# Linear attention block on one core: products of Wv with the state in two column tiles of TensorE

## The chip, the cores and the metric

The kernel runs on one core of one Trainium2 chip. The metric is the device time of one execution in microseconds (us); lower is better. A time given for a kernel is the median of several runs of it.

## The reference

x has 2048 rows of 640 columns, in bf16. There are 32 heads of 20 columns each. With phi(t) = (t + 1 if t > 0, else exp(t)) + 1e-6, the block computes, per head:

```
qkv = x @ wqkv                     # q, k, v: 640 columns each
pq, pk = phi(q), phi(k)
kv  = sum over rows of pk^T v      # 20 x 20 per head, the state
z   = sum over rows of pk          # 20 per head
o   = (pq @ kv) / (pq . z + 1e-6)
out = o @ wo                       # the heads side by side, 640 x 640
```

## The kernel before, in words

The kernel never forms v. Since v = x Wv, the state of all heads is Wv^T (x^T pk), of which only the 20 x 20 blocks on the diagonal are wanted. And since out = o wo, each head's state is multiplied with its 20 rows of wo once ("fold"), so that the end of the kernel is a single product of the normalized pq with a folded matrix of 640 x 640.

The stages on TensorE, in order:

1. Six products that only keep TensorE busy (L280), ten transposes of x (L198), then k = x Wk in 16 row tiles of 128 (L292). Exp on ScalarE (L305) and two operations on VectorE (L307, L310) make pk of it.
2. P = x^T pk (L319), 640 x 640, summed over the 16 row tiles, in two halves of 320 columns. Each half is copied out of PSUM into `pt` by ScalarE (L331) and VectorE (L334). In between stand tiles of q (L345), 20 in all, 128 columns by 512 rows of x each, with exp on ScalarE (L353) and two operations on VectorE (L357, L360) that make pq. VectorE also sums z (L366, L387), and the denominators' weighted sums (`wsum`, L412, four multiply-adds on VectorE behind one on ScalarE, L408, for each of the four blocks of 512 rows).
3. `kv_group` (L416, its products at L423): Wv^T P on the diagonal. The heads are taken in six groups `g`, five of six heads (GW = 120 columns) and one of two heads (40 columns). For each group five products are summed, one for each 128 rows of Wv: a weight of 128 x 128 (120 columns of Wv and 8 more), and 120 moving columns of `pt`. Groups 0 to 3 go to PSUM bank 0, groups 4 and 5 to bank 1.
4. `kv_mask` (L433, operations at L440): three VectorE operations multiply the results with a mask `bm` of diagonal blocks of 20 x 20 and write them as bf16 to `kvt`: groups 0 to 3 (480 columns), group 4 (120), group 5 (40).
5. `w2_group` (L444, products at L447), the fold: for each group two products of `kvt`'s 120 x 120 with the group's 120 rows of wo (`wog`), 320 columns each. A copy to `w2g` (L451) and a small DMA (L459) put the rows where the last stage wants them, in `w2p`.
6. The output (L487): pq times `w2p` for 16 row tiles, with the last denominators (`den`, L465; L470, L472) and normalizations (L479) in between, copies out of PSUM (L509, L512, L524), and the output DMAs.

The order on each engine is that of the program, written by hand. `P.add` records an operation for an engine with what it reads and writes. An operation waits, by semaphores, for the last writer of what it reads and for all readers of what it overwrites. The names count here, not the bytes: `("bank", b)` stands for a whole PSUM bank, `("kvt", g)` for one group. The product loop of one `P.add` signals once, with its last product. `next_q` issues a tile of q; an argument `between` is called after its exp was recorded and before its two VectorE operations, so that what it issues stands ahead of those in VectorE's queue and behind the tile's five products on TensorE. `todo` is a list of small operations (`work` fills it with weighted sums "w" and normalizations "n"), of which `pop` and `next_q(n)` take the next few. So around the state the order on TensorE is: tile of q, 30 products L423, tile of q, four products L447, tile of q, and so on. On VectorE it is: copies L334, three multiply-adds L412, three masks L440, then the two operations of the tile of q.

`pool_const` prepares constants on GpSimd (L167: zeros in `kvt`'s last group; L168: zeros in the last group of `wog`; the mask `bm` by two selections, L159). `load_rest` issues the DMA loads of Wq, x, Wv and wo (L260: five groups of 120 rows of wo) on SyncE's queue.

Of the kernel before, what the change touches and what calls it, by code (L numbers as in the profile page):

```python
# [7 lines left out]
ALU = mybir.AluOpType  # L8
# [74 lines left out]
def bass_standalone__linear_attn_block__prompt_kernel(nc, x, wqkv, wo, out):  # L83
    B, S, D = x.shape
    assert (B, S, D) == (1, 2048, 640)
    H, DH = 32, 20
    NC_ = D // 128
    NT = S // 128
    HALF = D // 2
    NSB = S // 512  # L90
    GW, NG = 120, 6
    gsz = [min(GW, D - GW * g) for g in range(NG)]
    BK = 512

    with contextlib.ExitStack() as ctx:
        es = ctx.enter_context

        def sb(name, cols, dt=BF16):
            return es(nc.sbuf_tensor(name, [128, cols], dt))
# [6 lines left out]
        wv = sb("wv", NC_ * D + 128)  # L106
        wog = sb("wog", NG * D)
# [4 lines left out]
        pt = sb("pt", NC_ * D)  # L112
        kvt = sb("kvt", NG * GW)
# [8 lines left out]
        bm = sb("bm", GW)  # L122
# [7 lines left out]
        ps = es(nc.psum_tensor("ps", [128, 8 * BK], F32))  # L130

        P = Plan(nc, es)

        def bank(b, n=BK, off=0, parts=128):
            return ps[0:parts, BK * b + off:BK * b + off + n]

        def two_banks(b, n=HALF, parts=128):
            return ps[0:parts, BK * b:BK * b + 2 * BK].rearrange(
                "p (g j) -> p g j", j=BK)[:, :, 0:n]

        def fold(ap, j=HALF):
            return ap.rearrange("p (g j) -> p g j", j=j)


        def pool_const():
            P.add("pool", lambda e: e.memset(ident[:, :], 0.0), writes=["ident"])
            P.add("pool", lambda e: e.affine_select(
                out=ident[:, :], in_=ident[:, :], pattern=[[-1, 128]], base=0,
                channel_multiplier=1, compare_op=ALU.not_equal, fill=1.0),
                reads=["ident"], writes=["ident"])  # L150
            P.add("dve", lambda e: e.memset(ones[:, :], 1.0), writes=["ones"])
            P.add("dve", lambda e: e.memset(eps[:, :], 1e-6), writes=["eps"])
            P.add("pool", lambda e: e.memset(wv[:, NC_ * D:], 0.0), writes=["wvpad"])
            P.add("pool", lambda e: e.memset(hm[:, :], 1.0), writes=["hm"])

            def band(t, pat, base, mult, name):

                v = t.rearrange("p (a b) -> p a b", b=pat[1][1])
                P.add("pool", lambda e: e.affine_select(  # L159
                    out=v, in_=v, pattern=pat, base=base, channel_multiplier=mult,  # L160
                    compare_op=ALU.is_ge, fill=0.0), reads=[name], writes=[name])


            band(hm[:, :], [[-4, 32], [0, 4]], 0, 1, "hm")
            band(hm[:, :], [[4, 32], [0, 4]], 3, -1, "hm")

            P.add("pool", lambda e: e.memset(kvt[:, 5 * GW:], 0.0), writes=[("kvt", 5)])  # L167
            P.add("pool", lambda e: e.memset(wog[:, 5 * D:], 0.0), writes=["wog5"])  # L168
            P.add("pool", lambda e: e.memset(bm[:, :], 1.0), writes=["bm"])
            for lo in (True, False):  # L170
                band(bm[:, :], [[-DH if lo else DH, NG], [0, DH]],
                     0 if lo else DH - 1, 1 if lo else -1, "bm")


        NPE = 2
# [48 lines left out]
        def w_cols(dst, lo, hi, col, key, eng):  # L224
            P.add(eng, lambda e: e.dma_start(
                dst[:, 0:NC_ * D].rearrange("p (c n) -> p c n", n=D)[:, :, lo:hi],
                wqkv[:, col + lo:col + hi].rearrange("(c p) n -> p c n", p=128)),
                writes=[key], dma=True)

        def load_xn(a, b, eng, reads=()):  # L230
            P.add(eng, lambda e: e.dma_start(
                xn[:, a * D:b * D].rearrange("p (t n) -> p t n", n=D),
                x[0, 128 * a:128 * b, :].rearrange("(t p) n -> p t n", p=128)),
                reads=reads, writes=[("xn", t) for t in range(a, b)], dma=True)
# [20 lines left out]
        def load_rest():  # L255
            w_cols(wqn, 0, D, 0, "wqn", "sp")
            for a, b in ((2, 6), (6, 11), (11, 16)):
                load_xn(a, b, "sp")
            w_cols(wv, 0, D, 2 * D, "wv", "sp")
            P.add("sp", lambda e: e.dma_start(  # L260
                wog[0:GW, 0:5 * D].rearrange("p (g n) -> p g n", n=D),
                wo[0:5 * GW, :].rearrange("(g p) n -> p g n", p=GW)),
                writes=["wog"], dma=True)
            P.add("sp", lambda e: e.dma_start(
                wog[0:gsz[5], 5 * D:6 * D], wo[5 * GW:D, :]), writes=["wog5"], dma=True)

# [148 lines left out]

        def kv_group(b):  # L416

            for lo, hi, bb in ((0, 4, b), (4, 6, b + 1)):
                def mm(e, lo=lo, hi=hi, bb=bb):
                    for g in range(lo, hi):  # L420
                        n = gsz[g]
                        for d in range(NC_):
                            r = e.matmul(  # L423
                                bank(bb, n, off=128 * (g - lo)),
                                wv[:, d * D + GW * g:d * D + GW * g + 128],
                                pt[:, d * D + GW * g:d * D + GW * g + n],
                                start=(d == 0), stop=(d == NC_ - 1))
                    return r
                P.add("pe", mm, reads=["wv", "wvpad"] + [("pt", d, h) for d in range(NC_)
                                                         for h in range(2)],  # L430
                      writes=[("bank", bb)])

        def kv_mask(b):  # L433
            for lo, n, bb, w in ((0, 4, b, GW), (4, 1, b + 1, GW), (5, 1, b + 1, 40)):
                src = ps[0:w, BK * bb + 128 * (lo % 4):BK * bb + 128 * (lo % 4) + 128 * n] \
                    .rearrange("p (g j) -> p g j", j=128)[:, :, 0:w]
                m = bm[0:w, 0:w].unsqueeze(1).broadcast_to([w, n, w])
                dst = kvt[0:w, GW * lo:GW * (lo + n)].rearrange(
                    "p (g j) -> p g j", j=GW)[:, :, 0:w]
                P.add("dve", lambda e, src=src, m=m, dst=dst: e.tensor_tensor(  # L440
                    dst, src, m, ALU.mult), reads=[("bank", bb), "bm"],
                    writes=[("kvt", g) for g in range(lo, lo + n)])

        def w2_group(g, b, eng="act"):  # L444
            n = gsz[g]
            for h in range(2):
                P.add("pe", lambda e, h=h: e.matmul(  # L447
                    bank(b + h, HALF, parts=GW), kvt[0:GW, GW * g:GW * (g + 1)],
                    wog[0:GW, g * D + HALF * h:g * D + HALF * (h + 1)], start=True, stop=True),
                    reads=[("kvt", g), "wog", "wog5"], writes=[("bank", b + h)])  # L450
            P.add(eng, lambda e: (e.copy if eng == "act" else e.tensor_copy)(  # L451
                fold(w2g[0:n, g * D:(g + 1) * D]), two_banks(b, parts=n)),
                reads=[("bank", b), ("bank", b + 1)], writes=[("w2g", g)])
            w2_rows(g)

        def w2_rows(g):

            w = gsz[g] // NC_
            P.add("sp", lambda e: e.dma_start(  # L459
                w2p[24 * g:24 * g + w, :].rearrange("p (c n) -> p c n", n=D),  # L460
                w2g[0:gsz[g], g * D:(g + 1) * D]),
                reads=[("w2g", g)], writes=[("w2p", g)], dma=True)
# [84 lines left out]
        for k in order.split():  # L547
            st = int(k[1])
# [20 lines left out]
        def take():  # L569
            small.append(small.pop(0))  # L570
            return small[-1]

        def next_q(n=1, between=None):
            q_tile(*qs.pop(0), take(), between)
            for _ in range(n):
                if todo:
                    todo.pop(0)()

        def inverse(s):
            b = take()  # L580
            den(s, b)
            den_act(s, b)
# [8 lines left out]
        def pop(n):  # L591
            for _ in range(n):
                todo.pop(0)()
# [15 lines left out]
        for st in range(NT - 2):  # L609
            p_step(1, st)  # L610
            if st in (0, 1):
                zst.pop(0)()
            if st == 5:
                z_finish(take())
                work("w0", "w1", "n0")
                pop(3)
            if st in (1, 4, 7, 10, 12):
                next_q({7: 2, 10: 2}.get(st, 0))
            if st == 11:
                inverse(0)  # L620
        assert not zst
# [1 line left out]
            p_step(1, NT - 2, (d,))  # L623
            p_step(1, NT - 1, (d,))
        p_out(1)
        pop(3)

        def state_groups():
            kv_group(0)
# [73 lines left out]
```

## Time and profile before

| | |
|---|---|
| median of 3 runs | 99.46 us (99.34 to 99.53) |
| the profiled execution | 99.4 us |
| its span, first to last instruction | 98.1 us |
| TensorE busy | 95.0 us (97% of the span) |
| VectorE busy | 74.0 us |
| ScalarE busy | 50.3 us |
| GpSimd busy | 3.5 us |
| mean granted TensorE clock | 1.000 |

Times within the trace count from the span's start. PE is TensorE's products, PEld its weight loads, DVE is VectorE, ACT ScalarE, POOL GpSimd, SPq SyncE's DMA queue. L423 is line 423 of the kernel. A product's record lasts longer than the step to the next product, since products follow each other through the array before the first has ended: for the time that a group of products takes on the engine, the steps from start to start count, not the records' lengths. Some records of products are missing from the trace (95 of 100 at L345, for instance).

### The profile page before, as it was taken

The numbers are of one execution on the slowest core, as the hardware profiler recorded it, in microseconds if no ns is written. First come the engines' busy times: TensorE is split into PE (matmuls) and PEld (weight loads), VectorE is DVE, ScalarE is ACT, GpSimd is POOL, SyncE is SP. The second block draws the span as 40 slices with busy tenths as digits, with TensorE's granted clock in tenths as the row PEclk, the third lists the DMA queues.
The fourth block names the chain that finished last, engine by engine and source line by source line (L and its number), as shares of the span: only waits on it lengthen the run. The fifth ranks groups of instructions, "written<-read, shape, count | busy, mean of one in ns | idle before, by whom it ended". The sixth has DMA issues, their size and how long they took to land.

```text
span 98.1 us, 1667 instructions
## 1 busy us (share of the span) xinstructions
PE 95.0 (97%) x651; PEld 62.4 (64%) x657; DVE 74.0 (75%) x138; ACT 50.3 (51%) x83; POOL 3.5 (4%) x15
## 2 busy tenths in 40 slices
PE   6999999999999999999999999999999999999991
PEld 2667777777777666555566556755447776677771
DVE  0305987888889897999849759999979998819332
ACT  5107454445698201462042476289796749665321
POOL 6800000000000000000000000000000000000000
DMA  2986899989999920000000000006600223322534
GB/s 47 361 193 131 162 169 135 218 272 379 366 362 284 205 63 10 0 0 0 0 7 0 0 0 0 0 0 165 164 15 0 98 102 134 134 70 73 197 134 134
DMA packets 17236, 11.73 MB, mean 120 GB/s; under 512 B 9933, under 2 KB 17229, under 8 KB 17229
## 3 DMA queue, kind: packets, MB, share of 16 engines
q1 hardware_dynamic: 16653, 11.10, 42.9%
q10 hardware_dynamic: 576, 0.53, 1.6%
q8 instruction: 5, 0.08, 0.4%
q14 instruction: 2, 0.02, 0.1%
HBM read 5.90 MB, written 2.62 MB: 87 GB/s over the span
## 4 chain that ended last, share of the span: by engine, by line
PE 90%; DVE 6%; ACT 1%; issue 0%
PE ps L292 23%; PE ps L487 22%; PE ps L345 21%; PE ps L319 17%; DVE za L366 3%; PE ps L280 3%; PE ps L447 2%; PE ps L423 1%; DVE pq L360 1%; ACT eq L353 1%; PE ps L198 1%; PE ps L465 1%; DVE eq L357 1%; DVE pt L334 0%; DVE osb L512 0%
## 5 line engine op out<-in xcount | busy, mean ns | idle before, releaser
L319 PE MATMUL ps<-pk,xn 128*128 128x320 bf16 x160 | 24.0, 299 | 0.0
L345 PE MATMUL ps<-xT,wqp 128*128 128x512 bf16 x95 | 23.1, 379 | 0.3
L292 PE MATMUL ps<-wk,xT 128*128 128x320 bf16 x160 | 22.9, 305 | 0.0
L487 PE MATMUL ps<-w2p,pq 128*128 128x320 bf16 (+3 forms) x170 | 22.3, 291 | 0.1
L353 ACT ACTIVATE eq<-ps 128x512 bf16<-128x512 f32 x20 | 11.9, 597 | 19.2 <-PE ps L345 19.0
L319 PEld LDWEIGHTS ps<-pk,xn 128*128 128x128 bf16 x160 | 15.6, 98 | 7.5
L292 PEld LDWEIGHTS ps<-wk,xT 128*128 128x128 bf16 x160 | 15.9, 100 | 6.5 <-ACT xT L210 0.2
L487 PEld LDWEIGHTS ps<-w2p,pq 128*128 128x128 bf16 x170 | 15.9, 98 | 6.4 <-DVE pq L479 0.2
L305 ACT ACTIVATE ek<-ps 128x640 bf16<-128x640 f32 x16 | 11.2, 704 | 11.8 <-PE ps L292 11.1
L345 PEld LDWEIGHTS ps<-xT,wqp 128*128 128x128 bf16 x100 | 9.7, 97 | 9.2
L360 DVE SCALAR_TENSOR_TENSOR pq<-ps,eq 128x512 bf16<-128x512 f32 x20 | 13.8, 692 | 0.7
L310 DVE SCALAR_TENSOR_TENSOR pk<-ps,ek 128x640 bf16<-128x640 f32 x16 | 13.2, 825 | 0.5
L412 DVE SCALAR_TENSOR_TENSOR ua<-pq,zc,ua 128x512 f32<-128x512 bf16 x12 | 9.0, 749 | 1.1 <-ACT ua L408 0.9
L307 DVE TENSOR_SCALAR ek<-ek 128x640 bf16<-128x640 bf16 x16 | 5.2, 324 | 5.9 <-ACT ek L305 5.9
L479 DVE TENSOR_TENSOR pq<-pq,rd 128x512 bf16<-128x512 bf16 x20 | 7.4, 418 | 2.8 <-ACT rd L472 2.8
L357 DVE TENSOR_SCALAR eq<-eq 128x512 bf16<-128x512 bf16 x20 | 5.8, 289 | 4.1 <-ACT eq L353 3.9
L524 ACT CAST osb<-ps 128x640 bf16<-128x640 f32 x9 | 6.2, 688 | 3.6 <-PE ps L487 3.4
L512 DVE CAST osb<-ps 128x320 bf16<-128x320 f32 (+2 forms) x8 | 3.5, 434 | 3.3 <-PE ps L487 3.1
L366 DVE TENSOR_TENSOR za<-pk 128x1280 f32<-128x1280 bf16 x4 | 5.8, 1483 | 0.0
L509 ACT CAST osb<-ps 128x320 bf16<-128x320 f32 (+1 forms) x8 | 3.1, 404 | 4.7 <-PE ps L487 4.5
L366 DVE TENSOR_TENSOR za<-za 128x1280 f32<-128x1280 f32 x3 | 4.4, 1482 | 0.0
L270 ACT COPY wqp<-wqn 128x640 bf16<-128x640 bf16 x5 | 4.3, 933 | 0.0
(41 smaller groups left out, 43.5 us busy)
## 6 DMA issues: line engine op xcount, KB each, us to landing
out_dram<-osb SPq DMA_DIRECT2D x15, 160.0 KB, 1.8
xn<-in_x_dram SPq DMA_DIRECT2D x2, 800.0 KB, 10.1
wqn<-in_wqkv_dram SPq DMA_DIRECT2D x1, 800.0 KB, 6.4
wv<-in_wqkv_dram SPq DMA_DIRECT2D x1, 800.0 KB, 13.6
wog<-in_wo_dram SPq DMA_DIRECT2D x1, 750.0 KB, 14.2
w2p<-w2g SPq DMA_DIRECT2D x5, 150.0 KB
xn<-in_x_dram SPq DMA_DIRECT2D x1, 640.0 KB, 7.6
wk<-in_wqkv_dram SPq DMA_DIRECT2D x3, 160.0 KB, 3.4
```

What stands on the lines that cost most here:

```text
L292: r = e.matmul(bank(b + h, HALF), xT[:, c * S + 128 * st:c * S + 128 * st + 128], wk[:, c * D + HALF * h:c * D + HALF * (h + 1)], start=(c ...
L305: P.add("act", lambda e: e.activation(fold(t[:, :]), two_banks(b), ACTF.Exp), reads=banks + ["table"], writes=[("ek", st % 3)])
L310: P.add("dve", lambda e: e.scalar_tensor_tensor(fold(pk[:, st * D:(st + 1) * D]), two_banks(b), 0.0, fold(t[:, :]), ALU.max, ALU.add), rea ...
L319: r = e.matmul(bank(d, HALF), xn[:, st * D + 128 * d:st * D + 128 * d + 128], pk[:, st * D + HALF * h:st * D + HALF * (h + 1)], start=(st ...
L345: r = e.matmul(bank(b), wqp[:, d * D + 128 * c:d * D + 128 * c + 128], xT[:, d * S + BK * sbk:d * S + BK * (sbk + 1)], start=(d == 0), sto ...
L353: P.add("act", lambda e: e.activation(t[:, :], bank(b), ACTF.Exp), reads=[("bank", b), "table"], writes=[("eq", i)])
L357: P.add("dve", lambda e: e.tensor_scalar(t[:, :], t[:, :], 1.0, 1e-6, ALU.min, ALU.add), reads=[("eq", i)], writes=[("eq", i)])
L360: P.add("dve", lambda e: e.scalar_tensor_tensor(pq[:, c * S + BK * sbk:c * S + BK * (sbk + 1)], bank(b), 0.0, t[:, :], ALU.max, ALU.add), ...
L366: P.add("dve", lambda e: e.tensor_tensor(d_ap, a, b, ALU.add), reads=ra + rb, writes=[dst])
L412: P.add("dve", lambda e: e.scalar_tensor_tensor(dst[:, :], v, z, a[:, :], ALU.mult, ALU.add), reads=[("pq", s, c), "zc", key], writes=[dkey])
L479: P.add("dve", lambda e: e.tensor_tensor(v, v, rd[i][:, BK * o:BK * (o + 1)], ALU.mult), reads=[("rd", sbk), ("pq", sbk, c)], writes=[("pq ...
L487: r = e.matmul(bank(b, hi - lo), pq[:, c * S + 128 * st:c * S + 128 * st + 128], w2p[:, c * D + lo:c * D + hi], start=(c == 0), stop=(c == ...
```

## The change

The products of Wv with the state are made in halves of the array. Each group of six heads is cut in two parts `t` of three heads, 60 columns. Part 0 takes 64 columns of weights and writes PSUM rows 0 to 63, part 1 takes 64 columns and writes rows 64 to 127; the moving operand is 60 columns of `pt`. The instructions alternate between the two parts. The last group of two heads has part 0 alone. So there are 55 products (50 with 60 columns, 5 with 40) in place of 30 (25 with 120, 5 with 40). All of them go to bank 0, 64 columns a group, in one recorded operation.

The mask operations become: part 0 of groups 0 to 4 (64 rows, 300 columns), part 1 of groups 0 to 4 (64 rows, 300 columns), group 5 (64 rows, 40 columns). Each of the first two writes part of every group 0 to 4.

`kvt` thus holds a group's heads in rows 0 to 59 and 64 to 123, and the fold's products sum over 128 rows in place of 120. `kvt` is zeroed as a whole at the start (720 columns in place of 120). `wog` is loaded in two DMAs of 64 rows in place of one of 120; the rows that belong to no head of the group meet zeros in `kvt`. The mask `bm` is made by two selections of the same size as before with another pattern.

One multiply-add of the weighted sums is issued earlier: three operations of `todo` instead of two behind the tile of q at step 10 of the second half of P, and two instead of three behind the copies of that half.

```diff
-            P.add("pool", lambda e: e.memset(kvt[:, 5 * GW:], 0.0), writes=[("kvt", 5)])
+            P.add("pool", lambda e: e.memset(kvt[:, :], 0.0),
+                  writes=[("kvt", g) for g in range(NG)])
...
-            P.add("sp", lambda e: e.dma_start(
-                wog[0:GW, 0:5 * D].rearrange("p (g n) -> p g n", n=D),
-                wo[0:5 * GW, :].rearrange("(g p) n -> p g n", p=GW)),
-                writes=["wog"], dma=True)
+            for t in range(2):
+                P.add("sp", lambda e, t=t: e.dma_start(
+                    wog[64 * t:64 * t + 64, 0:5 * D].rearrange("p (g n) -> p g n", n=D),
+                    wo[40 * t:40 * t + 5 * GW, :].rearrange("(g p) n -> p g n", p=GW)[
+                        20 * t:20 * t + 64]),
+                    writes=[("wog", t)], dma=True)
...
-            for lo, hi, bb in ((0, 4, b), (4, 6, b + 1)):
-                def mm(e, lo=lo, hi=hi, bb=bb):
-                    for g in range(lo, hi):
-                        n = gsz[g]
-                        for d in range(NC_):
+            def mm(e):
+                for g in range(NG):
+                    for d in range(NC_):
+                        for t in range(2 if g < 5 else 1):
+                            col = d * D + GW * g + 60 * t
+                            n = min(60, gsz[g])
                             r = e.matmul(
-                                bank(bb, n, off=128 * (g - lo)),
-                                wv[:, d * D + GW * g:d * D + GW * g + 128],
-                                pt[:, d * D + GW * g:d * D + GW * g + n],
+                                ps[64 * t:64 * t + 64, BK * b + 64 * g:BK * b + 64 * g + n],
+                                wv[:, col:col + 64], pt[:, col:col + n],
                                 start=(d == 0), stop=(d == NC_ - 1))
...
-            for lo, n, bb, w in ((0, 4, b, GW), (4, 1, b + 1, GW), (5, 1, b + 1, 40)):
+            for lo, n, t, w in ((0, 5, 0, 60), (0, 5, 1, 60), (5, 1, 0, 40)):
+                p = slice(64 * t, 64 * t + 64)
...
                 P.add("pe", lambda e, h=h: e.matmul(
-                    bank(b + h, HALF, parts=GW), kvt[0:GW, GW * g:GW * (g + 1)],
-                    wog[0:GW, g * D + HALF * h:g * D + HALF * (h + 1)], start=True, stop=True),
+                    bank(b + h, HALF, parts=GW), kvt[:, GW * g:GW * (g + 1)],
+                    wog[:, g * D + HALF * h:g * D + HALF * (h + 1)], start=True, stop=True),
...
-                next_q({7: 2, 10: 2}.get(st, 0))
+                next_q({7: 2, 10: 3}.get(st, 0))
...
         p_out(1)
-        pop(3)
+        pop(2)
```

More of the change, by code (lines that the diff above doesn't have):

```diff
@@ L165, in pool_const @@
             band(hm[:, :], [[4, 32], [0, 4]], 3, -1, "hm")
-            P.add("pool", lambda e: e.memset(kvt[:, 5 * GW:], 0.0), writes=[("kvt", 5)])
+            P.add("pool", lambda e: e.memset(kvt[:, :], 0.0),
+                  writes=[("kvt", g) for g in range(NG)])
             P.add("pool", lambda e: e.memset(wog[:, 5 * D:], 0.0), writes=["wog5"])
             P.add("pool", lambda e: e.memset(bm[:, :], 1.0), writes=["bm"])
-            for lo in (True, False):
-                band(bm[:, :], [[-DH if lo else DH, NG], [0, DH]],
-                     0 if lo else DH - 1, 1 if lo else -1, "bm")
+            for lo in (1, -1):
+                P.add("pool", lambda e, lo=lo: e.affine_select(
+                    out=bm.rearrange("p (t b j) -> p t b j", b=3, j=DH),
+                    in_=bm.rearrange("p (t b j) -> p t b j", b=3, j=DH),
+                    pattern=[[-64 * lo, 2], [-DH * lo, 3], [0, DH]],
+                    base=0 if lo > 0 else DH - 1, channel_multiplier=lo,
+                    compare_op=ALU.is_ge, fill=0.0), reads=["bm"], writes=["bm"])
         NPE = 2
@@ L423, in mm @@
                             r = e.matmul(
-                                bank(bb, n, off=128 * (g - lo)),
-                                wv[:, d * D + GW * g:d * D + GW * g + 128],
-                                pt[:, d * D + GW * g:d * D + GW * g + n],
+                                ps[64 * t:64 * t + 64, BK * b + 64 * g:BK * b + 64 * g + n],
+                                wv[:, col:col + 64], pt[:, col:col + n],
                                 start=(d == 0), stop=(d == NC_ - 1))
-                    return r
@@ L429, in kv_group @@
-                P.add("pe", mm, reads=["wv", "wvpad"] + [("pt", d, h) for d in range(NC_)
-                                                         for h in range(2)],
-                      writes=[("bank", bb)])
+                return r
+            P.add("pe", mm, reads=["wv", "wvpad"] + [("pt", d, h) for d in range(NC_)
+                                                     for h in range(2)],
+                  writes=[("bank", b)])
         def kv_mask(b):
-            for lo, n, bb, w in ((0, 4, b, GW), (4, 1, b + 1, GW), (5, 1, b + 1, 40)):
[L435 to L439, printed above, removed]
+            for lo, n, t, w in ((0, 5, 0, 60), (0, 5, 1, 60), (5, 1, 0, 40)):
+                p = slice(64 * t, 64 * t + 64)
+                src = ps[p, BK * b + 64 * lo:BK * b + 64 * (lo + n)] \
+                    .rearrange("p (g j) -> p g j", j=64)[:, :, 0:w]
+                m = bm[p, 60 * t:60 * t + w].unsqueeze(1).broadcast_to([64, n, w])
+                dst = kvt[p, GW * lo:GW * (lo + n)].rearrange(
+                    "p (g j) -> p g j", j=GW)[:, :, 60 * t:60 * t + w]
@@ L440, in kv_mask @@
                 P.add("dve", lambda e, src=src, m=m, dst=dst: e.tensor_tensor(
-                    dst, src, m, ALU.mult), reads=[("bank", bb), "bm"],
+                    dst, src, m, ALU.mult), reads=[("bank", b), "bm"],
                     writes=[("kvt", g) for g in range(lo, lo + n)])
@@ L447, in w2_group @@
                 P.add("pe", lambda e, h=h: e.matmul(
-                    bank(b + h, HALF, parts=GW), kvt[0:GW, GW * g:GW * (g + 1)],
-                    wog[0:GW, g * D + HALF * h:g * D + HALF * (h + 1)], start=True, stop=True),
-                    reads=[("kvt", g), "wog", "wog5"], writes=[("bank", b + h)])
+                    bank(b + h, HALF, parts=GW), kvt[:, GW * g:GW * (g + 1)],
+                    wog[:, g * D + HALF * h:g * D + HALF * (h + 1)], start=True, stop=True),
+                    reads=[("kvt", g), ("wog", 0), ("wog", 1), "wog5"],
+                    writes=[("bank", b + h)])
             P.add(eng, lambda e: (e.copy if eng == "act" else e.tensor_copy)(
```

## The prediction

> **What bounds the kernel now.** I read the page's busy shares and its chain first, then the waits from 57 us on (TensorE's alone), then a table of two stretches, columns as in the heading that I keep: length, and busy time of each engine.
>
> ```profile
> PE 95.0 (97%) x651; PEld 62.4 (64%) x657; DVE 74.0 (75%) x138; ACT 50.3 (51%) x83; POOL 3.5 (4%) x15
> PE 90%; DVE 6%; ACT 1%; issue 0%
> ```
> ```profile
> PEld ps L447 <- DVE kvt L440: 0.2, 1, 0.2
> PEld ps L487 <- DVE pq L479: 0.2, 1, 0.2
> ```
> ```profile
> core 0: us, PE busy (x) PEld busy (x) DVE busy (x) ACT busy (x) POOL busy (x), PEclk, DMA share, GB/s
> 4.40:96.20 91.80, 91.44 (x638) 60.63 (x641) 73.06 (x134) 48.88 (x82) 0.23 (x1) 1.00 0.44 115
> ```
>
> TensorE is the chain: 91.44 of 91.80 us busy between the first product of k and the last output tile, at a clock of 1.00, and the remainder is about what five product records missing at L345 would fill. Only weight loads ever wait, 0.2 us each, beside products still running. So whatever the state's stage takes or gives on TensorE moves everything after it, unless VectorE makes the next stage wait. Now the stage itself, in the timeline (start, length, engine):
>
> ```profile
> 59.91 1.03 PE L345 MATMUL ps<-xT,wqp 128*128 128x512 bf16 x4
> 60.22 1.53 DVE L412 SCALAR_TENSOR_TENSOR ua<-pq,zc,ua 128x512 f32<-128x512 bf16 x2
> 60.78 1.59 PE L423 MATMUL ps<-pt,wv 128*128 128x120 bf16 x30
> 61.79 0.75 DVE L412 SCALAR_TENSOR_TENSOR ub<-pq,zc,ua 128x512 bf16<-128x512 bf16 x1
> 62.22 1.24 PE L345 MATMUL ps<-xT,wqp 128*128 128x512 bf16 x5
> 62.46 0.94 DVE L440 TENSOR_TENSOR kvt<-ps,bm 120x480 bf16<-120x480 f32 x3
> 63.16 0.54 PEld L447 LDWEIGHTS ps<-wog,kvt 120*120 120x120 bf16 x4 [0.20 <-DVE kvt L440]
> 63.30 0.71 PE L447 MATMUL ps<-wog,kvt 120*120 120x320 bf16 x4
> 63.32 0.28 DVE L357 TENSOR_SCALAR eq<-eq 128x512 bf16<-128x512 bf16 x1
> ```
>
> The 30 products hold TensorE from 60.78 to 62.22: **1.44 us**, all that there is to win. Five products of a tile of q follow, until 63.30, and the fold's first product starts at 63.30. The masks start at 62.46, when the third multiply-add ends. So two clocks meet at 63.30 with nothing to spare: TensorE's queue, and masks plus weight load.
>
> **The change part by part.** *Steps of products.* Records overlap, so I take steps from the chain (start, length) and from two rows of the timeline around the one-column products of L397.
>
> ```profile
> 52.05 2.04 PE ps L319 x15
> ...
> 70.71 3.24 PE ps L345 x15
> ```
> ```profile
> 49.33 0.27 PE L397 MATMUL ps<-ones,zs 128*128 128x1 bf16 x5
> 49.46 0.84 PE L319 MATMUL ps<-pk,xn 128*128 128x320 bf16 x5
> ```
>
> 512 columns step in 3.24/15 = 216 ns, 320 in 136 ns: 0.417 ns a column and 2.7 ns. That gives 27.7 ns for 60 columns and 52.7 for 120. One column takes (49.46 - 49.33)/5 = 26 ns, so 26 ns is the least step seen. Before: 25 x 52.7 + 5 x 26 = 1.45 us, as measured. After, in two bounds:
> - The two parts run **at the same time**: 25 pairs at 27.7 ns and five products at 26 ns, 0.82 us. Saving 0.62.
> - They run **one after the other**: 50 x 27.7 + 5 x 26 = 1.52 us. Loss 0.08.
>
> No record shows two parts of the array at work, so the trace doesn't choose. The 26 ns for one column, each with a weight load of its own between, show that loads stream ahead of products; the two parts share no weights and no PSUM rows. I take the pairs as simultaneous, near to even odds.
>
> [...]
>
> *Going into and out of halves.* No row has that. Lower bound: nothing. Upper bound: the array empties each time, from these groups by form (line, engine, shapes, count, busy us, mean ns):
>
> ```profile
> L345 PE MATMUL ps<-xT,wqp 128*128 128x512 bf16 x95 | 23.1, 379 | 0.3
> L345 PEld LDWEIGHTS ps<-xT,wqp 128*128 128x128 bf16 x100 | 9.7, 97 | 9.2
> L440 DVE TENSOR_TENSOR kvt<-ps,bm 120x480 bf16<-120x480 f32 x1 | 0.7, 650 | 0.0
> L423 PE MATMUL ps<-pt,wv 128*128 128x40 bf16 x5 | 0.3, 180 | 0.0
> L440 DVE TENSOR_TENSOR kvt<-ps,bm 120x120 bf16<-120x120 f32 x1 | 0.3, 272 | 0.0
> L440 DVE TENSOR_TENSOR kvt<-ps,bm 40x40 bf16<-40x40 f32 x1 | 0.2, 181 | 0.0
> ```
>
> In: the tail of a tile-of-q product, 379 - 216 = 163 ns, then a load of 97 ns: 0.26 us. Out: 180 - 26 = 154 ns and 97 ns: 0.25 us. I take half of each, 0.13 and 0.13. [...]
>
> *Masks.* 650 ns for 480 columns and 272 for 120: 1.05 ns a column, so 461 ns for 300. The three take 63.32 - 62.46 = 0.86 us with records of 1.10 in sum: each starts 81 ns ahead of its predecessor's end, a step of 380 ns. Sum after: 0.38 + 0.38 + 0.11, the same 0.86. But all wait for one bank, that is for the last of 55 products, and the fold's first group needs both large masks: 0.38 + 0.46 = 0.84 us from mask start to `kvt` ready, against 0.65. This added wait holds behind it on VectorE the tile of q's two operations, which start at 63.32 now and would not be later.
>
> *The multiply-add moved up.* VectorE's part of the timeline:
>
> ```profile
> 56.77 0.74 DVE L412 SCALAR_TENSOR_TENSOR ua<-pq,zc,ua 128x512 f32<-128x512 bf16 x1
> 58.49 0.29 DVE L357 TENSOR_SCALAR eq<-eq 128x512 bf16<-128x512 bf16 x1 [0.97 <-ACT eq L353]
> ```
>
> It goes into an idle 0.97 us ahead of 58.49 and needs 0.78 (a step, from two in 60.22 to 61.79): hidden, 0.19 to spare. Without that cover it would push the copies to `pt`, at most 0.78. After it, VectorE is free at 61.79 in place of 62.46.
>
> *The sum.* With X the stage's length and E the price of going in, the masks start at the later of 61.79 and 60.78 + E + X - 0.03 + 0.18 + 0.02 = 60.95 + E + X: last product's start, its 180 ns, and 0.02 to the consumer (this step in the chain):
>
> ```profile
> 57.84 0.02 issue
> 57.86 0.60 ACT eq L353
> ```
>
> Then 0.84 us of masks, 0.05 to the weight load (63.11 to 63.16) and 0.14 to the first product (63.16 to 63.30): **fold at 61.98 + E + X by VectorE**. By TensorE it is at 60.78 + E + X + out + 1.08. With X = 0.82, E = out = 0.13: masks at 61.90, fold at 62.93 by VectorE, 62.94 by TensorE. Against 63.30 that is **0.37 us earlier**; VectorE's masks end 0.56 earlier, so later stages follow. Gain reaches the end one for one, since TensorE has no idle time later that would take it up. The profiled execution took 99.4, 0.06 below the median of 99.46: 99.4 - 0.37 = 99.03, or 99.09 on the median's scale. Break-even is E + X = 1.32, 48 ns a pair with E at nothing.
>
> *Costed at nothing*: the second DMA for wo, the longer fill of `kvt`, 128 rows in place of 120 in the fold (columns set its step).
>
> ```profile
> 23.73 2.12 SPq L260 DMA_DIRECT2D wog<-in_wo_dram  x1
> 25.89 1.85 SPq L264 DMA_DIRECT2D wog<-in_wo_dram  x1
> ```
> ```profile
> 64.70 5.29 SPq L459 DMA_DIRECT2D w2p<-w2g  x6
> ```
> ```profile
> L168 POOL MEMSET wog<- 128x640 bf16 x1 | 0.6, 631 | 0.0
> L167 POOL MEMSET kvt<- 128x120 bf16 x1 | 0.2, 198 | 0.0
> ```
>
> One more issue on SyncE, some 2 us, falls into the time from 27.74 to 64.70 in which its queue issues nothing; what is queued behind it are the DMAs at L264 and L459. The fill grows by 600 columns at (631 - 198)/520 = 0.83 ns, 0.5 us, and holds up only GpSimd's own constants, which the masks first need at 62.46. Without those covers: 2 us and 0.5 us.
>
> **The rivals.**
> - **B, side by side, but the array empties at both ends.** E = 0.26, out = 0.25: fold by TensorE at 60.78 + 0.26 + 0.82 + 0.25 + 1.08 = 63.19, 0.11 early, 99.35. For: nothing in the trace changes the shape, so the price may be whole. Against: weight loads and products of other lines change over without a gap.
> - **C, the parts don't run side by side** (the change doesn't do what it says), at no price at the ends. X = 1.43 to 1.52: fold by VectorE at 63.41 to 63.50, 0.11 to 0.20 late, about 99.6. For: one-column products step no faster than 26 ns.
> - **D, slower: one after the other, and the array empties.** Fold by TensorE at 60.78 + 0.26 + 1.52 + 0.25 + 1.08 = 63.89, 0.59 late: 100.05. It decides as soon as E + X exceeds 1.32, by VectorE's path, or E + X + out 1.44 by TensorE's.
> - **E, weight loads of 64 columns come out into the open.** If each of 55 products had to wait for its own load of 97 ns, X would be 5.3 us and the time near 103.4; a third of that, 1.8 us, gives 99.46 + 0.48. For: a load's record of 97 ns is longer than the step of a pair. Against: it is longer than the step of 52.7 ns now, too, and lies wholly beside products.
>
> **How the numbers follow.** Forecast (A) 99.1, chance 0.45; nearly all of it is faster by over 0.2%, which is 0.2 us and about what a measurement of this kernel can tell. B 0.12, same. C 0.13, mostly same. D 0.23 and E 0.07, slower. So faster 0.43, same 0.22, slower 0.35. The range: its low end is A with free ends, where masks at 61.79 put the fold at 62.81, 0.49 early, 98.97, less 0.07, within the spread of 0.1 to either side that the three runs of before have: 98.9. Its high end takes in D: 100.1. As both signs are likely, A's own range: 98.9 to 99.3.
>
> **What would show it.** In the changed profile: 55 products in about 0.82 us (pairs a few ns apart, 28 ns from pair to pair) for A and B, steps of 26 to 28 ns for C and D; a gap ahead of the first and behind the last for B and D; masks of 0.46 us starting near 61.9; the first fold product near 62.9, its load ended by L440's second operation; the moved multiply-add ended before 58.49. I am wrong if products step evenly at 26 ns or more, if the gaps at the ends exceed 0.5 us, or if a later product of L487 waits for VectorE and gives the gain back.

## The result and the profile after

| | before | after |
|---|---|---|
| median of 16 runs each, us | 99.40 (99.05 to 99.81) | 99.03 (98.60 to 99.45) |
| ratio | | 0.9958, 95% interval 0.9939 to 0.9978 |
| the profiled execution, its span, us | 99.4, 98.1 | 98.91, 97.6 |

In this measurement the kernel after is 0.37 us faster; the forecast was 99.1 us, 0.37 us faster. The trace shows how much of that is the change. First the page of the kernel after (busy time of the engines, and the chain), and TensorE's waits from 57 us on:

```profile
PE 94.7 (97%) x682; PEld 61.5 (63%) x682; DVE 74.2 (76%) x138; ACT 50.3 (52%) x83; POOL 4.0 (4%) x15
PE 92%; DMA 4%; SPq 1%; issue 0%; DVE 0%
```
```profile
PEld ps L431 <- issue: 0.4, 1, 0.4
PEld ps L455 <- DVE kvt L448: 0.4, 1, 0.4
PEld ps L496 <- DVE pq L488: 0.2, 1, 0.2
```

TensorE is still the chain. Three weight loads wait now in place of two. New is the wait of the first one of the products in halves (for nothing that the profile shows); the first of the fold waits 0.4 us for the masks in place of 0.2; the last is as before. The stage in the timeline of the kernel after (L431 are the products, L448 the masks, L455 the fold, L419 the multiply-adds, L352 the tile of q):

```profile
57.23 0.75 DVE L419 SCALAR_TENSOR_TENSOR ua<-pq,zc,ua 128x512 f32<-128x512 bf16 x1
58.17 0.29 DVE L364 TENSOR_SCALAR eq<-eq 128x512 bf16<-128x512 bf16 x1 [0.19 <-ACT eq L360]
...
59.25 0.88 PEld L352 LDWEIGHTS ps<-xT,wqp 128*128 128x128 bf16 x5
...
60.55 1.13 PE L431 MATMUL ps<-pt,wv 128*64 128x60 bf16 x55
...
60.68 0.75 DVE L419 SCALAR_TENSOR_TENSOR ub<-pq,zc,ua 128x512 bf16<-128x512 bf16 x1
61.61 0.76 PEld L352 LDWEIGHTS ps<-xT,wqp 128*128 128x128 bf16 x5
...
61.71 1.19 DVE L448 TENSOR_TENSOR kvt<-ps,bm 64x300 bf16<-64x300 f32 x3 [0.28 <-PE ps L431]
62.73 0.46 PEld L455 LDWEIGHTS ps<-wog,kvt 128*120 128x120 bf16 x4 [0.37 <-DVE kvt L448]
62.74 0.75 PE L455 MATMUL ps<-wog,kvt 128*120 128x320 bf16 x4
62.83 0.28 DVE L364 TENSOR_SCALAR eq<-eq 128x512 bf16<-128x512 bf16 x1
```

The 55 products run from 60.55 to the next weight load at 61.61, 1.06 us. Product by product, the two of a pair start some 4 ns apart, and from pair to pair it is 31.7 ns. The multiply-add moved up ended ahead of 58.17. To compare two traces past an early shift, I count from the first weight load of the tile of q ahead of the state's products. Three marks of the weight-load timeline for before, after, and the kernel after once more (run `again`): P's first products, that tile of q, and the output stage.

```profile
11.76 0.23 PEld L319 LDWEIGHTS ps<-pk,xn 128*128 128x128 bf16 x2
59.56 0.88 PEld L345 LDWEIGHTS ps<-xT,wqp 128*128 128x128 bf16 x5
73.57 0.86 PEld L487 LDWEIGHTS ps<-w2p,pq 128*128 128x128 bf16 x6
```
```profile
11.44 0.23 PEld L326 LDWEIGHTS ps<-pk,xn 128*128 128x128 bf16 x2
59.25 0.88 PEld L352 LDWEIGHTS ps<-xT,wqp 128*128 128x128 bf16 x5
73.05 1.40 PEld L496 LDWEIGHTS ps<-w2p,pq 128*128 128x128 bf16 x10
```
```profile
11.82 0.23 PEld L326 LDWEIGHTS ps<-pk,xn 128*128 128x128 bf16 x2
59.63 0.88 PEld L352 LDWEIGHTS ps<-xT,wqp 128*128 128x128 bf16 x5
73.44 0.99 PEld L496 LDWEIGHTS ps<-w2p,pq 128*128 128x128 bf16 x7
```

From the first mark to the second it is 47.80 to 47.81 us in all three. From the second to the third it is 14.01 before and 13.80 and 13.81 after: **0.21 us, that is what the changed stage is worth**, and to the last output tiles it stays 0.21. The other 0.32 us by which the two profiles differ lie ahead of P's first products, in the kernel's first 12 us.

### The profile page after: what moved, and what is told of

It is laid out like the page before. It is cut to its first block, busy times and chain, and to the rows that moved or that the text cites. A ratio compares the mean times of both kernels' runs of the same rounds, so it can differ in the third digit from the quotient of the medians.

```text
span 97.6 us, 1725 instructions
## 1 busy us (share of the span) xinstructions
PE 94.7 (97%) x682; PEld 61.5 (63%) x682; DVE 74.2 (76%) x138; ACT 50.3 (52%) x83; POOL 4.0 (4%) x15
## 4 chain that ended last, share of the span: by engine, by line
PE 92%; DMA 4%; SPq 1%; issue 0%; DVE 0%
PE ps L496 22%; PE ps L326 22%; PE ps L352 22%; PE ps L299 21%; DMA wk<-in_wqkv_dram 4%; PE ps L455 2%; PE ps L431 1%; PE ps L474 1%; SPq L252 0%; SPq L236 0%; DVE osb L521 0%; PE ps L404 0%
## 5 line engine op out<-in xcount | busy, mean ns | idle before, releaser
L352 PE MATMUL ps<-xT,wqp 128*128 128x512 bf16 x100 | 24.2, 379 | 0.0
L352 PEld LDWEIGHTS ps<-xT,wqp 128*128 128x128 bf16 x100 | 9.7, 98 | 9.2
L419 DVE SCALAR_TENSOR_TENSOR ua<-pq,zc,ua 128x512 f32<-128x512 bf16 x12 | 9.0, 749 | 1.1 <-ACT ua L415 0.9
```

Source lines behind the costliest of these rows:

```text
L352: r = e.matmul(bank(b), wqp[:, d * D + 128 * c:d * D + 128 * c + 128], xT[:, d * S + BK * sbk:d * S + BK * (sbk + 1)], start=(d == 0), sto ...
L419: P.add("dve", lambda e: e.scalar_tensor_tensor(dst[:, :], v, z, a[:, :], ALU.mult, ALU.add), reads=[("pq", s, c), "zc", key], writes=[dkey])
```

## The experiments

The theory: two halves side by side shorten TensorE's stage by 0.27 to 0.28 us; 0.07 of that goes back to the wait for the masks; the early 0.32 us are scatter. The rivals: the gain is VectorE's (the move), or comes from cheap products of 64 columns in any place, or from the start. "Stage" is the time from the tile of q's first weight load to that of the output stage, as above, from each run's trace; it repeats to 0.01 us. The measured ratios are far coarser.

| run | stage, us | against before | P's first products at | ratio to before, 95% interval |
|---|---|---|---|---|
| before | 14.01 | | 11.76 | |
| after | 13.80 | -0.21 | 11.44 | 0.9958, 0.9939 to 0.9978 |
| again | 13.81 | -0.21 | 11.82 | 0.9986, 0.9956 to 1.0016 |
| move_only | 14.01 | 0.00 | 12.07 | 1.0003, 0.9974 to 1.0033 |
| tiles_only | 14.22 | +0.21 | 12.12 | 1.0048, 1.0022 to 1.0074 |
| part_by_part | 13.81 | -0.21 | 11.42 | 0.9995, 0.9970 to 1.0020 |
| half_g5 | 14.25 | +0.24 | 11.89 | 1.0021, 1.0000 to 1.0043 |
| start_only | 14.01 | 0.00 | 11.38 | 1.0008, 0.9987 to 1.0030 |
| two_banks | 13.79 | -0.22 | 12.08 | 0.9983, 0.9959 to 1.0007 |
| two_banks_w60 | 13.79 | -0.22 | 11.47 | 0.9983, 0.9962 to 1.0004 |
| one_half | 14.51 | +0.50 | 11.67 | 1.0050, 1.0023 to 1.0077 |
| parts_apart | 14.50 | +0.49 | 12.13 | 1.0056, 1.0028 to 1.0084 |
| two_banks_late | 14.67 | +0.66 | 11.72 | 1.0031, 1.0011 to 1.0052 |
| two_banks_spread | 13.67 | -0.34 | 12.16 | 0.9994, 0.9969 to 1.0018 |

**again**, the kernel after once more.

> The changed kernel once more, beside the kernel before on the same chip. Theory (the stage of the Wv products is shorter by 0.28 us on TensorE, and 0.08 us of that goes back to a wait for the masks; the 0.32 us by which the k stage was shorter in the one profile is scatter of the start): from the first weight load of the stage's tile of q to the last stage the shift against before is again 0.21 us, while the start of P's first products (11.76 us before, 11.44 after) falls anywhere; time 0.2% under before. Rival (something in the change makes the start faster each time): the start of P's first products is again near 11.44 us, time 0.5% under before.

The stage repeats; P's first products come at 11.82, later than in the profile of before. **start_only** is the kernel before with the early part of the change:

```diff
-P.add("pool", lambda e: e.memset(kvt[:, 5 * GW:], 0.0), writes=[("kvt", 5)])
+P.add("pool", lambda e: e.memset(kvt[:, :], 0.0), writes=[("kvt", g) for g in range(NG)])
...
-    wog[0:GW, 0:5 * D].rearrange("p (g n) -> p g n", n=D),
-    wo[0:5 * GW, :].rearrange("(g p) n -> p g n", p=GW)),
+    wog[60 * t:60 * t + 60, 0:5 * D].rearrange("p (g n) -> p g n", n=D),
+    wo[0:5 * GW, :].rearrange("(g p) n -> p g n", p=GW)[60 * t:60 * t + 60]),
```

> The kernel before with only what the change does early: kvt zeroed as a whole, wo loaded in two DMAs (of 60 rows each). Theory (the shorter k stage in the one profile of the changed kernel was scatter): within 0.1% of before, and the start of P's first products anywhere between 11.3 and 11.9 us. Rival (this part of the change makes the start faster): 0.2% to 0.3% under before, P's first products near 11.44 us.

Stage 0.00, time unchanged within its interval. Its profile has P's first products at 11.38, but kernels with all that the change does early have them at 11.44, 11.82 and 12.12, and one without any early part (move_only) at 12.07: a scatter of 0.78 us over all runs that follows no edit. So the start is not part of the gain.

The traces show where it scatters. The first products of k step 267 ns from start to start, later ones 136 ns, and the point at which the step halves differs from execution to execution: behind five products in before, one in after, seven in move_only, none in start_only. A stretch of 0.80 us in before, then the same in after (columns as in the prediction's table, but PE and PEld alone, and k alone; in brackets the records that touch the stretch):

```profile
4.70:5.50 0.80, 0.80 (x5) 0.42 (x4) 1.00 1.10 354
```
```profile
4.70:5.50 0.80, 0.80 (x8) 0.54 (x6) 1.00 1.08 363
```

Before loses 5 x 0.131 + 0.03 = 0.69 us to this. After loses 0.12, and 0.24 around a wait for a DMA of wk that comes next: 0.36, and the difference is the 0.32 us. The column of the clock shows 1.00 in both stretches, so it does not tell the two steps apart.

**move_only** and **tiles_only**: the change in its two pieces. move_only is the kernel before with the edit below; tiles_only is the changed kernel with this edit undone.

```diff
-next_q({7: 2, 10: 2}.get(st, 0))
+next_q({7: 2, 10: 3}.get(st, 0))
...
-pop(3)
+pop(2)
```

> The kernel before with the multiply-add moved up, products and masks as before. Theory (TensorE sets the end, and the fold's start at 63.30 was set by TensorE's queue as well as by the masks): masks start near 62.03 instead of 62.46, as soon as the products of bank 0 are done, the fold's first product at the same place in TensorE's queue; time within 0.1% of before. Rival (the gain of the change is VectorE's, by the earlier masks): 0.2% to 0.4% under before.

> The changed kernel without the move: three multiply-adds ahead of the masks, as before. Theory: VectorE gets free 0.78 us later than in the changed kernel (61.43 there), near 62.2 on its clock, so the masks start 0.5 us later and the fold 0.5 us later: 0.3 us (0.3%) over before, and the whole gain of the products is lost in a wait of the fold's first weight load for the masks. Rival (the move hides nothing that matters): the same time as the changed kernel.

Alone, the move brings nothing (14.01): the masks start 0.43 us earlier, but the fold stays behind TensorE's own queue. Without the move, the kernel loses 0.42 us against after and is slower than before. In the timeline of tiles_only, fold load and fold wait for the masks, which wait for VectorE's third multiply-add:

```profile
62.83 1.18 DVE L448 TENSOR_TENSOR kvt<-ps,bm 64x300 bf16<-64x300 f32 x3
63.84 0.46 PEld L455 LDWEIGHTS ps<-wog,kvt 128*120 128x120 bf16 x4 [0.79 <-DVE kvt L448]
63.84 0.75 PE L455 MATMUL ps<-wog,kvt 128*120 128x320 bf16 x4 [0.29 <-DVE kvt L448]
```

The direction was expected, 0.3 us; it was 0.21.

**part_by_part**: the loops of `t` and `d` exchanged.

```diff
-for d in range(NC_):
-    for t in range(2 if g < 5 else 1):
+for t in range(2 if g < 5 else 1):
+    for d in range(NC_):
```

> The changed kernel with the five products of part 0 of a group ahead of the five of part 1, in place of alternating. Theory (two parts side by side take one step of 31.7 ns together, and a part alone takes the same step): 55 steps of 31.7 ns in place of 30, 0.79 us more on TensorE, and the fold 0.58 us later than before: 0.6% over before. Rival (half arrays with 64 columns of weights are cheap by themselves, or TensorE reorders across parts): the same time as the changed kernel.

My theory fell here as I had put it: nothing was lost. Records do not say which half a product is in, but in part_by_part some 25 of the 55 products start 5 ns behind another, and in one_half, below, none starts less than 31 ns behind another. The products take as long as in after: 61.59 - 60.53 = 1.06 us from the first weight load to the tile of q's. So TensorE paired products of the two halves against the program's order. The rival named two causes, so two more runs separate them. **one_half** puts part 1 into the same half of the array, in another bank; **parts_apart** orders all of part 0 ahead of all of part 1.

```diff
-ps[64 * t:64 * t + 64, BK * b + 64 * g:BK * b + 64 * g + n],
+ps[0:64, BK * (b + t) + 64 * g:BK * (b + t) + 64 * g + n],
```
```diff
-for g in range(NG):
-    for d in range(NC_):
-        for t in range(2 if g < 5 else 1):
+for t in range(2):
+    for g in range(NG if t == 0 else 5):
+        for d in range(NC_):
```

> The changed kernel with both parts in the same half of the array: all 55 products write PSUM rows 0 to 63, part 1 to bank 1, and its masks write the state to rows 0 to 63 of the second columns, so that part 1's heads meet the wrong rows of wo (this part of the computation is changed; every operation has the size of the changed kernel's). Theory (a half steps at 31.7 ns by itself, and the gain is that two halves work at a time; with the parts' products in blocks of five, TensorE still ran both halves at once): 55 steps of 31.7 ns, the stage 0.79 us longer than in the changed kernel, the end 0.58 us later than before. Rival (products of 64 columns of weights are cheap wherever they stand): the stage as in the changed kernel, the end 0.21 us earlier.

> The changed kernel with all 30 products of part 0 (groups 0 to 5) ahead of all 25 of part 1. Theory (each half takes its products in order, and TensorE looks ahead over at least some 10 products, since blocks of five cost nothing): if it sees 30 or more products ahead, the stage is as long as in the changed kernel, 30 steps of 31.7 ns; if it sees only N ahead, part 1 starts when 30 - N of part 0 are done, and the stage is (30 - N) steps longer at most: for N = 10, 20 steps or 0.63 us, the end 0.4 us later than before. Rival (it looks ahead over blocks of five and not over more): 25 steps or 0.79 us longer.

The timeline of one_half, and of parts_apart (weight loads of the products, of the tile of q behind them; masks):

```profile
60.78 1.81 PEld L431 LDWEIGHTS ps<-pt,wv 128*64 128x64 bf16 x55 [0.42 <-issue]
62.63 0.55 PEld L352 LDWEIGHTS ps<-xT,wqp 128*128 128x128 bf16 x4
62.74 0.95 DVE L448 TENSOR_TENSOR kvt<-ps,bm 64x300 bf16<-64x300 f32 x3 [1.07 <-PE ps L431]
```
```profile
61.24 1.72 PEld L431 LDWEIGHTS ps<-pt,wv 128*64 128x64 bf16 x55 [0.42 <-issue]
62.99 0.11 PEld L352 LDWEIGHTS ps<-xT,wqp 128*128 128x128 bf16 x2
63.10 1.19 DVE L448 TENSOR_TENSOR kvt<-ps,bm 64x300 bf16<-64x300 f32 x3 [0.98 <-PE ps L431]
```

In one half the stage takes 62.63 - 60.78 = 1.85 us in place of 1.06: 25 steps more for 0.79 us, 31.6 ns each. Two products of 64 weight columns in one half thus take 63 ns, more than the 52.7 ns of the one product that they replace; the gain is that two halves work at a time. The output stage comes 0.50 us later than before, where 0.58 was expected: the masks, all in the same rows here, give some 0.08 back (more on this below). Apart, it takes 1.75: 22 steps more. So only three of 25 products of part 1 ran beside part 0, where I had expected at least ten. That is near the rival's 25. TensorE did take products of the other half out of order, but here only some three products ahead; that blocks of five still fit into this is how I read part_by_part, where all pairs formed.

**half_g5**: the kernel before with its last group alone in a half, to price the way in and out.

```diff
+w = 64 if g == 5 else 128
-bank(bb, n, off=128 * (g - lo)),
-wv[:, d * D + GW * g:d * D + GW * g + 128],
+bank(bb, n, off=128 * (g - lo), parts=w),
+wv[:, d * D + GW * g:d * D + GW * g + w],
```

> The kernel before with its last group (two heads, five products) in 64 columns of weights and 64 rows of PSUM, the other 25 products in the full array: one change into halves and one out, and no two parts side by side. Theory (going in costs 0.11 us and going out 0.10 us, whatever is done in between): the five products step at 31.7 ns in place of 26, and the tile of q behind the stage starts 0.24 us later; 0.2% over before. Rival (the gap ahead of the first product in halves comes from the wait for the state's copies, and the gap behind from nothing that repeats): the tile of q 0.03 us later, within 0.1%.

As expected: stage 0.24 us longer, of which five products stepping at 31.7 in place of 26 ns are 0.03. In and out of halves costs 0.21 us. The weight loads of the two tiles of q around the products, in half_g5:

```profile
59.70 0.23 PEld L345 LDWEIGHTS ps<-xT,wqp 128*128 128x128 bf16 x2
```
```profile
62.58 0.76 PEld L345 LDWEIGHTS ps<-xT,wqp 128*128 128x128 bf16 x5
```

2.88 us apart, in place of 62.20 - 59.56 = 2.64 before (the second load in the timeline of before stands at 62.20).

**two_banks**, **two_banks_w60**: the wait for the masks, and what sets the step.

```diff
-def mm(e):
-    for g in range(NG):
+for lo, hi, bb in ((0, 2, b), (2, NG, b + 1)):
+    def mm(e, lo=lo, hi=hi, bb=bb):
+        for g in range(lo, hi):
...
-for lo, n, t, w in ((0, 5, 0, 60), (0, 5, 1, 60), (5, 1, 0, 40)):
+for lo, n, t, w in ((0, 2, 0, 60), (0, 2, 1, 60),
+                    (2, 3, 0, 60), (2, 3, 1, 60), (5, 1, 0, 40)):
```

two_banks_w60 has 60 in place of 64 columns of weights and rows of PSUM, too.

> The changed kernel with groups 0 and 1 in bank 0 and groups 2 to 5 in bank 1, each recorded by itself, and the masks in five operations (two of 120 columns, two of 180, one of 40). Theory (the fold's first weight load waits for two masks of 300 columns that start only when all 55 products are done): the masks start when VectorE gets free, 0.28 us earlier, the fold's first group is ready before TensorE gets to it, and the wait of 0.08 us goes: 0.3% under before. Rival (five masks cost VectorE more than they free, and it is late for the tile of q): not under the changed kernel.

> The kernel with two banks, and 60 columns of weights in place of 64 for each part (PSUM rows 0 to 59 and 64 to 123). Theory (the step of a pair, 31.7 ns with 60 and with 40 moving columns alike, is set by the weight load, one array cycle of 0.42 ns a column): a step of 30.0 ns, 0.05 us less for the 30 steps, 0.05% more gained. Rival (a fixed floor of a half's step): 31.7 ns as before.

The wait for the masks went, and 60 columns took 0.05 us off the 30 steps: 61.59 - 60.59 = 1.00 us from first load to the tile of q's, in place of 1.06. But the stage gained only 0.01 in all. The timeline of two_banks_w60 shows where the rest was given back, in the third line's wait:

```profile
60.59 0.97 PEld L432 LDWEIGHTS ps<-pt,wv 128*60 128x60 bf16 x55 [0.42 <-issue]
61.59 0.76 PEld L352 LDWEIGHTS ps<-xT,wqp 128*128 128x128 bf16 x5
...
64.65 0.18 PEld L459 LDWEIGHTS ps<-wog,kvt 128*120 128x120 bf16 x2 [0.21 <-DVE w2g L464]
```

The fold of group 3 needs banks 0 and 1, which VectorE is still copying group 1 out of. Two cures. **two_banks_late** (on two_banks_w60) frees VectorE early; **two_banks_spread** puts a tile of q between.

```diff
-        pop(2)
...
-        pop(3)
+        pop(5)
```
```diff
         w2_group(2, 2)
-        w2_group(3, 0)
         next_q(0)
-        w2_group(4, 2)
+        w2_group(3, 0)
         next_q(1)
-        w2_group(5, 0)
+        w2_group(4, 2)
         next_q(1)
+        w2_group(5, 0)
         next_q(1)
```

> The kernel with two banks and 60 columns of weights, and the two multiply-adds that stood ahead of the masks put behind the tile of q that follows the first fold groups. Theory (with two banks and 60 columns the stage gains 0.11 us more by the second block of the fold, 0.33 in all, but loses 0.11 of it there, as the fold of group 3 waits until VectorE has copied group 1 out of the same banks): VectorE is free 1.5 us earlier, masks of groups 0 and 1 start when bank 0 is done, the copy of group 1 ends some 0.2 us earlier, and the end is 0.33 us earlier than before instead of 0.22. Rival (VectorE's whole queue is what limits from here on): 0.22 us earlier as before, the wait found at another place.

> The kernel with two banks and 60 columns of weights, with the fold of groups 3, 4 and 5 one tile of q later each, multiply-adds as in the changed kernel. Theory (there the fold of group 3 waits 0.11 us until VectorE has copied group 1 out of banks 0 and 1; a tile of q, 1.08 us, covers that wait, and VectorE's queue is in the same order as there): the end 0.33 us earlier than before in the trace, in place of 0.22; 0.3% under before. Rival (VectorE's queue is late by then, too): TensorE loses 0.11 us or more at a tile of q, waiting for a bank, and the end is 0.22 us earlier or less.

two_banks_late removed that wait and lost 1 us behind it. Its masks waited 1.09 us for the products, time that the two multiply-adds had filled, and they came back when tiles of q needed banks (TensorE's waits):

```profile
PEld ps L352 <- DVE pq L367: 2.2, 4, 0.8
```

So the rival's cause was right, VectorE's queue is close behind TensorE; its time was not: 0.22 us under before was said, and 0.66 over it was measured. two_banks_spread did as expected, weight loads of the tile of q and of the output stage 13.67 us apart:

```profile
59.97 0.88 PEld L352 LDWEIGHTS ps<-xT,wqp 128*128 128x128 bf16 x5
73.64 0.86 PEld L500 LDWEIGHTS ps<-w2p,pq 128*128 128x128 bf16 x6
```

By its trace it is the shortest, 0.34 us under before and 0.13 under after. Its measured ratio, 0.9994 with an interval of 0.9969 to 1.0018, does not show it: the start scatters by more than twice that (P's first products at 12.16 us in its profile).

## Why the prediction came out, point by point

**Bound: right.** TensorE without idle time passes on what the stage gives: 0.21 us at the fold's second block, at the output stage and at the last tiles alike.

**Side by side: right** (A, not C or D), though held at near even odds. one_half shows it by its opposite.

**Step of a pair: too small.** Taken 27.7 ns for a pair and 26 for a single product, from the step of moving columns. It is 31.7 for both (25 steps in 0.79 us), whether 60 or 40 columns move (the last five products, with 40, start 31 to 32 ns apart), and 30.0 with 60 columns of weights ((1.06 - 1.00)/30 less, by the trace 1.6 ns). So the step went with the number of weight columns (64, then 60) and not with that of moving columns. Four columns fewer saved 1.6 ns, 0.4 ns each; the 0.42 expected was an estimate, from the 0.417 ns of a moving column. That the weight load sets the step is the likely reading and not shown by itself, since two_banks_w60 writes fewer rows of PSUM, too. The load's record in the kernel after, between loads of 128 and of 120 columns in the full array:

```profile
L352 PEld LDWEIGHTS ps<-xT,wqp 128*128 128x128 bf16 x100 | 9.7, 98 | 9.2
L431 PEld LDWEIGHTS ps<-pt,wv 128*64 128x64 bf16 x55 | 1.0, 112 | 0.4 <-issue 0.4
L455 PEld LDWEIGHTS ps<-wog,kvt 128*120 128x120 bf16 x12 | 1.4, 132 | 1.1 <-DVE kvt L448 0.4
```

Half as many columns take longer to load, 112 ns against 98. That it is the half that makes the load longer is not shown: the third row, 120 columns outside any half, takes 132 ns. Cost of the error: 25 x 4.0 + 5 x 5.7 = 0.13 us. The least step of 26 ns, which rival C rested on, did not hold across two halves: two products start 4 ns apart, and 55 take 30 steps.

**Ways in and out: about right.** 0.26 us taken, 0.21 measured. Whether the array empties is not shown; the price is under half of the upper bound of 0.51. TensorE's stage thus saved 0.27 us (2.63 to 2.36 between the tiles of q, before rounding) where 0.36 was forecast.

**Masks: the sum was mis-sized.** Their records were as worked out (461 ns taken):

```profile
L448 DVE TENSOR_TENSOR kvt<-ps,bm 64x300 bf16<-64x300 f32 x2 | 0.9, 468 | 0.3 <-PE ps L431 0.3
L448 DVE TENSOR_TENSOR kvt<-ps,bm 64x40 bf16<-64x40 f32 x1 | 0.2, 192 | 0.0
```

But the three took 62.83 - 61.71 = 1.12 us where 0.86 was taken. Each should have started 81 ns ahead of its predecessor's end; it started some 31 ns behind it (1.19 - 2 x 0.468 - 0.192 = 0.06 us for two gaps). In one_half, with all three in rows 0 to 63, the same shapes take 0.95 from first start to last end, against 1.19 in after and parts_apart, where the rows alternate. So it is the change of rows, not the shape. one_half changes the bank from mask to mask, too, but the bank is not it: in before, the second and third mask read the same bank, and both pairs overlap (records of 1.10 us in sum take 0.94); and in two_banks the third of five masks changes rows and bank and starts as late as the others. Its five records sum to 1.43 us, and they take 1.55:

```profile
61.99 1.55 DVE L452 TENSOR_TENSOR kvt<-ps,bm 64x120 bf16<-64x120 f32 x5
```

That made VectorE the later of the two clocks, and the fold stalled 0.07 us.

**The move: right that it was hidden**; its worth was left unsaid. Without it the change would have lost 0.21 us.

**Costed at nothing: right.** start_only has the second DMA for wo and the longer fill, and its stage stays at 14.01. The median record of the fold's products is 299 ns with 128 rows and 298 with 120.

**The total.** 0.37 was forecast and 0.37 measured, but the stage gives 0.21. Three measurements of that same stage (after, again, part_by_part) average (0.9958 + 0.9986 + 0.9995)/3 = 0.9980, 0.20 us; the intervals of the second and third include 1, so by time alone they show no gain. The trace's 0.21 of 99.4 is a ratio of 0.9979, just above the upper end of the first interval, 0.9978. So that 0.37 met 0.37 is luck: side, mechanism and place are right, the gain is a bit over half of the forecast. The rest of the first measured difference is most likely scatter, which the traces place ahead of P's first products, at the point where k's steps halve. What moves that point stays open.

## What to carry to other kernels

Two halves of TensorE pay for small products only as far as their steps allow: price a pair by its weight columns (here 31.7 ns for 64, 30.0 for 60), add the way in and out (0.21 us), and keep the two halves' products within a few of each other in the queue (blocks of five cost nothing, 30 ahead of 25 cost 22 steps). Where an engine without slack gets shorter, look at once at what is second: here the masks took back 0.07 us, with two banks a copy took 0.12 (13.79 against 13.67), and one multiply-add in the wrong place 0.42, twice the gain. When a run scatters by more than the change, count from a fixed mark ahead of the changed stage to one behind it; that repeats to 0.01 us where the time doesn't to 0.3.

## What the runs showed of the hardware, unexpected

- TensorE ran products of the two halves out of the program's order (part_by_part: 30 steps for 55 products, 1.06 us), with all of one half first about three products ahead (parts_apart: 52 steps, 1.75 us).
- Two VectorE operations in a row that changed from rows 0 to 63 to rows 64 to 127 or back lost the overlap of some 80 ns that they had in the same rows (1.19 against 0.95 us for three), whether they read the same bank or not (two_banks).
- The time to P's first products varies by 0.78 us between executions at a mean clock of 1.00, with no edit to show for it. k's first products step 267 ns and later ones 136, and the point of change wanders (behind one product in after, five in before, seven in move_only).
